# A fused top-k attention and two-MoE kernel: w_k loaded into w_v's later buffers, first loads on two queues, stand-in values from ScalarE

## The chip, the core and the metric

The kernel runs on one core of a Trainium2 chip. A core has five engines that work side by side: PE (TensorE, matrix products; PEld is its weight load), DVE (VectorE), ACT (ScalarE), POOL (GpSimd) and SP (SyncE, which here only issues DMAs). Each engine runs its own instructions strictly in order and waits on semaphores for the others. The metric is the device time in microseconds, the median of several runs.

## What is computed

```python
# 1. attention with top-k 32:  q, k, v are (4, 8, 576, 64)
scores = scale * q @ k.T                      # 576 scores a row
kth    = the 32nd largest of each row
attn   = softmax(where(scores >= kth, scores, -1e9)) @ v
# 2. x = attn as (4, 576, 512); each token is mixed with the one before it (mu_k, mu_r)
r, kk = sigmoid(xr @ w_r), relu(xk @ w_k) ** 2        # w_k 512x1024, w_v 1024x512, w_r 512x512
x = r * (kk @ w_v)
# 3. a routed MoE: each token goes to one of 8 experts (w1[e] 512x1024, w2[e] 1024x512)
out[b, s] = p[e] * (relu(x[b, s] @ w1[e]) @ w2[e])
```

w_k, w_v and w_r come as 64-bit floats; the kernel turns them into two 32-bit parts itself.

## The kernel before

The 2,304 tokens are 18 tiles of 128. A tile has 8 heads, worked off as 4 pairs of heads, so there are 72 **pairs** (`pair`, from L480). One pair with its two heads a = 0, 1 goes: PE scores (L511 or L516), ACT copies them out of PSUM (L498), DVE finds the eight largest of each of 8 blocks of 72 (L534) and three rounds of candidates (L544, L547); that gives an approximate threshold. Then the exact one is settled. DVE counts the scores below it into `sm` and writes the 0/1 mask `mk` (`cn`, L566). POOL does two things (`rp`): L570 writes eight **stand-in values** behind the mask (2^24 where a fixed number in `pick` exceeds the count, else 0), and L571 multiplies scores and mask. DVE takes the eight largest of these 584 numbers (`rx`, L575), and the eighth is the threshold whatever the count was. The stand-ins thus fill up the places that the count left open. ACT makes the final mask (L581), POOL subtracts it (L585), ACT takes exp (L589), PE transposes (L612), ACT copies (L615), PE multiplies with v (L625).

Between the pairs stand the first MoE (`mix`, `moe`; L823 to L947, in groups of two tiles) and, at the beginning, the conversion of the weights (`narrow`, from L684): 20 pieces of 128x512 64-bit numbers, 512 KB each, 8 of w_k, 4 of w_r, 8 of w_v. One piece is a DMA on SP's queue (L735) into a buffer `rw`, of which there are two, which it shares with other work; two ACT operations on it (L696, L711), four of DVE (L699 to L708), one or two of POOL, three PE products and two ACT copies into the final `wk` or `wv` buffer. There are eight `wk` and eight `wv` buffers.

After the pairs comes the second MoE (`slots`, up to L1826): a routing on DVE, PE and POOL (L1359), gathers of token rows by POOL (L1720), transposes (L1734), ACT and DVE splits into `xk` (L1737, L1740), expert products (L1758 or L1768, then L1808), with expert weights split into two parts by ACT, DVE and POOL (L1699, L1697, L1702), and scatters of the results (L1819).

What sets the order: every operation is handed to a planner (`Sched`, L35 to L143) with an estimated duration, a priority and the buffers it needs. It plays the program through with these estimates and emits each engine's instructions in the order in which they would start. The tables SHIFT, SLOPE and SCALE (L240 to L317) change priorities and durations by kind of operation; a kind is named by engine and function (`"ACT pair.ex"`). On the chip an engine keeps the emitted order, so an operation that is late holds up all behind it. While PE has nothing to do in the first 150 planned microseconds the planner puts in small products of no use (L1856), which keep PE running.

Of the kernel before, what the change touches and what calls it, by code (L numbers as in the profile page):

```python
# [146 lines left out]
def kernel(  # L147
# [92 lines left out]
    SHIFT = {"ACT Routing.own.<lambda>": 1600.4, "ACT keys.hi": -8273.1, "ACT mix.o1": -201.7, "ACT mix.o3": -55.0,  # L240
             "ACT moe.ev": -9550.0, "ACT moe.hi": -95.1, "ACT moe.rc": 2604.1, "ACT moe.rl": -1080.6,
             "ACT moe.sig": 9217.2, "ACT moe.sq": -2233.7, "ACT narrow.hi_": -6878.4, "ACT narrow.lo_": -3354.4,
             "ACT narrow.o1": -12605.5, "ACT narrow.o4b": 7243.4, "ACT narrow.o8": 82.5, "ACT pair.<lambda>": -3944.7,
             "ACT pair.cnt": 213.0, "ACT pair.cp": 153.5, "ACT pair.ev": -1356.5, "ACT pair.ex": 943.6,
             "ACT pair.ex2": 235.0, "ACT pair.nm": 645.5, "ACT pair.rl": -2339.7, "ACT queries.hi": -1850.3,
             "ACT slots.fin": -1800.3, "ACT slots.rl": 1990.9, "ACT slots.thi": -2317.5, "ACT slots.xhi": -8276.7,
             "ACT split.hi": 4421.4, "ACT x0_t.cs": -8538.1, "ACT x0_t.ev": -41.7,
             "DVE Routing.__init__.<lambda>": -8985.9, "DVE Routing.own.<lambda>": -2828.9,
             "DVE Routing.place.<lambda>": 1634.7, "DVE Routing.place.counts": -7047.9,
             "DVE Routing.place.order": 5600.6, "DVE Routing.place.rows": 2003.5, "DVE keys.lo": -172.9,  # L250
             "DVE mix.o1": 544.4, "DVE mix.o2": -1964.2, "DVE moe.lc": -7257.5, "DVE moe.lo": 12.5,
             "DVE moe.xs": 162.4, "DVE narrow.o1b": -1351.0, "DVE narrow.o2": 483.8, "DVE narrow.o3": 375.2,
             "DVE narrow.o4": -257.8, "DVE narrow.o9": 203.0, "DVE pair.cands": 3976.7, "DVE pair.ch": -3687.6,
             "DVE pair.cn": -78.5, "DVE pair.nm": -41.5, "DVE pair.r1": -646.5, "DVE pair.rx": -109.0,
# [1673 lines left out]
```

## Time and profile before

| | |
|---|---|
| median of 3 runs | 1061.44 us (1056.66 to 1063.55) |
| profiled execution | 1057.62 us, its span 1055.8 us |
| busy in the span | PE 988.2, DVE 880.2, ACT 778.6, POOL 754.4 us |
| pairs | from about 22 us (first L534) to about 700 us |
| routing of the second MoE | about 722 to 800 us |

The span runs from the first to the last instruction; 1.8 us lie around it. "Busy" is the time in which an engine had at least one instruction running. Idle time of an engine matters only where that engine, or one that waits for it, sets the end.

### The profile page before, as it was taken

Reading aid. Unit: us, or ns where it says so; the run is one execution under the profiler, and the core shown is the slowest. Engines: PE = TensorE matmul, PEld = TensorE weight load, DVE = VectorE, ACT = ScalarE, POOL = GpSimd, SP = SyncE. Lnnn points to the kernel's source line nnn. Section 1 sums busy time; section 2 is a strip of 40 time slices with the busy share of each in tenths; the row PEclk is TensorE's granted clock in tenths of the full one; section 3 lists DMA queues with packets and bytes.
Section 4 is the critical chain, followed back from the end, with each engine's and each line's share of the span. In section 5 each row is a group of like instructions: output and inputs, shape, how many; then the busy total and the mean of one; then the engine's idle time right before and its main releaser. Section 6 shows DMA issues by size and latency. Waiting matters only on the chain.

```text
span 1055.8 us, 24502 instructions
## 1 busy us (share of the span) xinstructions
PE 988.2 (94%) x7790; PEld 827.2 (78%) x7790; DVE 880.2 (83%) x3589; ACT 778.6 (74%) x1763; POOL 754.4 (71%) x858
## 2 busy tenths in 40 slices
PE   7898998899999999999999999999859999999896
PEld 6687884678787788888888788877759889888784
DVE  4998997858999999999989999958695669777672
ACT  4776786976999989989989799885335566566452
POOL 2686986666898989989978899873356757566552
PEclk9999999999999999999999999999789999999898
DMA  7421123234212353221342211003813646666650
GB/s 182 123 56 54 54 62 96 62 82 104 61 44 70 93 132 81 49 66 37 91 103 70 66 42 41 22 1 112 287 51 116 226 150 230 217 206 202 207 182 19
DMA packets 100974, 109.49 MB, mean 104 GB/s; under 512 B 49374, under 2 KB 67806, under 8 KB 100832
## 3 DMA queue, kind: packets, MB, share of 16 engines
q1 hardware_dynamic: 97312, 97.32, 32.4%
q0 software_dynamic: 3520, 10.49, 2.9%
q8 instruction: 64, 1.05, 0.4%
q14 instruction: 78, 0.64, 0.2%
HBM read 76.57 MB, written 10.49 MB: 82 GB/s over the span
## 4 chain that ended last, share of the span: by engine, by line
PE 58%; DVE 21%; ACT 8%; DMA 6%; issue 4%; SPq 0%; POOL 0%; POOLq 0%; DVEq 0%; ACTq 0%
PE pv L1808 9%; PE pb L1758 9%; PE xa L625 6%; PE pv L916 5%; PE pb L888 5%; PE pb L612 5%; DVE c L534 4%; PE pb L516 4%; PE pb L823 3%; DVE c L575 2%; PE pb L1768 2%; DVE mk L566 2%; PE pb L511 2%; PE pv L1856 2%; DMA rw<-in_moe_w_k_dram 2%
## 5 line engine op out<-in xcount | busy, mean ns | idle before, releaser
L585 POOL TENSOR_TENSOR at<-s,at 128x576 f32<-128x576 f32 x144 | 205.0, 1435 | 31.0 <-ACT at L581 30.4
L571 POOL TENSOR_TENSOR mk<-s,mk 128x576 f32<-128x576 f32 x144 | 205.6, 1428 | 0.0
L534 DVE MAX8 c<-s 128x8 f32<-128x72 f32 x1152 | 166.5, 219 | 4.8 <-ACT s L498 4.8
L581 ACT ACTIVATE at<-s,TS 128x576 f32<-128x576 f32 x144 | 112.1, 783 | 16.2 <-DVE TS L578 15.8
L1758 PE MATMUL pb<-xk,wk 128*128 128x256 f32 x864 | 114.6, 289 | 7.2 <-DVE xk L1740 7.2
L1758 PEld LDWEIGHTS pb<-xk,wk 128*128 128x128 f32 x864 | 112.3, 196 | 10.7 <-DVE xk L1740 7.5
L575 DVE MAX8 c<-mk 128x8 f32<-128x584 f32 x144 | 108.4, 757 | 14.6 <-POOL mk L571 14.6
L589 ACT ACTIVATE at<-at,sm 128x576 f32<-128x576 f32 x144 | 113.0, 786 | 7.7 <-POOL at L585 7.3
L498 ACT ACTIVATE s<-pb 128x288 f32<-128x288 f32 (+1 forms) x320 | 110.1, 418 | 8.4 <-PE pb L516 4.5
L612 PE MATMUL pb<-ident,at 128*128 128x128 f32 x648 | 99.1, 281 | 17.0 <-ACT at L589 11.8
L566 DVE TENSOR_SCALAR_CACHE_REDUCE mk<-s,c 128x576 f32<-128x576 f32 x144 | 114.8, 801 | 0.0
L615 ACT ACTIVATE aT<-pb 128x384 f32<-128x384 f32 x216 | 98.5, 497 | 12.7 <-PE pb L612 12.1
L916 PE MATMUL pv<-wv,kk 128*128 128x512 f32 x384 | 106.5, 406 | 0.0
L888 PE MATMUL pb<-xk,wk 128*128 128x256 f32 x768 | 103.9, 286 | 0.0
L612 PEld LDWEIGHTS pb<-ident,at 128*128 128x128 f32 x648 | 74.0, 142 | 37.5 <-ACT at L589 17.7
L625 PE MATMUL xa<-aT,vb 128*64 128x128 f32 (+1 forms) x1600 | 98.6, 269 | 2.4 <-ACT aT L615 1.8
L888 PEld LDWEIGHTS pb<-xk,wk 128*128 128x128 f32 x768 | 95.2, 188 | 2.9 <-issue 1.4
L625 PEld LDWEIGHTS xa<-aT,vb 128*64 128x64 f32 x1600 | 80.8, 138 | 19.2 <-issue 11.1
L1808 PE MATMUL pv<-wv,vb 128*128 128x512 f32 x330 | 88.5, 402 | 0.9 <-ACT xT L1816 0.9
L516 PE MATMUL pb<-kT,qx 128*128 128x288 f32 x480 | 86.5, 314 | 1.4 <-DMA kT<-rw 0.8
L1702 DVE TENSOR_TENSOR wk<-s,wk 128x512 fp32r<-128x512 f32 x67 | 70.7, 1088 | 16.1 <-ACT wk L1699 8.9
L516 PEld LDWEIGHTS pb<-kT,qx 128*128 128x128 f32 x480 | 69.6, 188 | 13.3 <-issue 5.3
(258 smaller groups left out, 2232.1 us busy)
## 6 DMA issues: line engine op xcount, KB each, us to landing
s<-in_moe_w_dram SPq DMA_DIRECT2D x88, 256.0 KB, 4.1
kT<-in_moe_w_dram SPq DMA_DIRECT2D x44, 512.0 KB, 5.1
qx<-qh SPq DMA_DIRECT2D x112, 64.0 KB, 2.0
qx<-ql SPq DMA_DIRECT2D x112, 64.0 KB, 2.0
kT<-rw SPq DMA_DIRECT2D x48, 144.0 KB, 2.6
xd<-rr SPq DMA_DIRECT2D x18, 256.0 KB, 2.2
rw<-in_moe_w_k_dram SPq DMA_DIRECT2D x8, 512.0 KB, 4.8
qn<-in_q_dram SPq DMA_DIRECT2D x16, 256.0 KB, 3.1
```

The lines of the kernel that those rows point to most:

```text
L516: nc.tensor.matmul(dst(hf), qx.t[:, w, a, hp % 2, :], kt.t[:, a, c], start=(w == 0), stop=(w == 1))
L534: nc.vector.max(c8.t[:, a, c, :], s2.t[:, c * CH:(c + 1) * CH])
L566: nc.vector.tensor_scalar(mk.t[:, :S], s2.t, c8.t[:, a, NCH + 2, 7:8], 0.0, op0=OP.is_lt, op1=OP.add, accum_out=sm.t[:, 2 + a:3 + a])
L571: nc.gpsimd.tensor_tensor(mk.t[:, :S], s2.t, mk.t[:, :S], op=OP.mult)
L575: nc.vector.max(c8.t[:, a, 0, :], mk.t)
L585: nc.gpsimd.tensor_tensor(x, s2.t, x, op=OP.subtract)
L612: nc.tensor.transpose(pt.t[:, c * P:(c + 1) * P], at.t[:, (g * GB + c) * P:(g * GB + c + 1) * P], ident)
L625: nc.tensor.matmul(xa.t[a * D:(a + 1) * D, hp * P + p0:hp * P + p0 + n], vb[:, a, j, :], evs[c // GB][1].t[:, c % GB, p0:p0 + n], start=(j ...
L888: nc.tensor.matmul(pm.t[:, :N], WK[c][f // 4].t[:, x, f % 4 * P:(f % 4 + 1) * P], xk.t[:, y, c, :N], start=(m == 0), stop=(m == 3 * DC - 1))
L916: nc.tensor.matmul(pvs[ti].t, kk.t[:, x, ti * P:(ti + 1) * P], WV[f].t[:, y, :], start=(f == 0 and m == 0), stop=(f == FB - 1 and m == 2))
L1758: nc.tensor.matmul(ph.t[:, (f % 2) * N:(f % 2 + 1) * N], w[:, x], xt.t[:, y, c, :], start=(n == 0), stop=(n == 3 * DC - 1))
L1808: nc.tensor.matmul(py.t, hT.t[:, x, o_:o_ + P], w[0].t[:, y, :], start=(f == 0 and m == 0), stop=(f == FC - 1 and m == 2))
```

## The change

Four edits, one of them in the tables.

1. The 8 pieces of w_k no longer go through the two `rw` buffers. They are loaded into the eight `wv` buffers (`RAWK`), which get w_v's converted pieces later; each `wv` buffer is free for w_v when the conversion of its w_k piece has read it. The planner now takes 4.0 us (it was 2.3) for a `narrow` load to land.
2. Of the first loads, the first tile of q (L450) and the second head of the first two heads of k (L387, L388 for h = 1) are issued from ACT's queue; all others stay on SP's.
3. The stand-in values are no longer made by POOL but by ACT (`si`, L583): Relu(STAND - count * STAND / (pick - 0.5)), which is positive where the count is below `pick`, with STAND 2^40. The constants are made once by four small DVE instructions (L356 to L359). DVE's L588 (L575 before) now waits for both ACT's `si` and POOL's product.
4. SHIFT, SLOPE and SCALE have new numbers for nearly every kind of operation, so that the order of all engines is laid anew.

```diff
-    HUGE, STAND = 2.0 ** 100, 2.0 ** 24
+    HUGE, STAND = 2.0 ** 100, 2.0 ** 40
-    SHIFT = {"ACT Routing.own.<lambda>": 1600.4, "ACT keys.hi": -8273.1, "ACT mix.o1": -201.7, "ACT mix.o3": -55.0,
+    SHIFT = {"ACT Routing.own.<lambda>": 560.7, "ACT keys.hi": -7234.3, "ACT mix.o1": -201.7, "ACT mix.o3": -55.0,
...
     WK = [[new("wk", [P, 2, 512], F32R) for _ in range(2)] for _ in range(DC)]
+
+    RAWK = [new("wv", [P, 2, DM]) for _ in range(2 * DC)]
     WV = [new("wv", [P, 2, DM], F32R) for _ in range(FB)]
...
-    pick = wp.tile([P, 8], F32, name="pick")
-    nc.gpsimd.iota(pick, pattern=[[-1, 8]], base=S - TOPK + 8, channel_multiplier=0, allow_small_or_imprecise_dtypes=True)
+    pick = wp.tile([P, 9], F32, name="pick")
+    nc.gpsimd.iota(pick[:, :8], pattern=[[-1, 8]], base=S - TOPK + 8, channel_multiplier=0, allow_small_or_imprecise_dtypes=True)
+    nc.vector.tensor_scalar(pick[:, :8], pick[:, :8], -0.5, None, op0=OP.add)
+    nc.vector.reciprocal(pick[:, :8], pick[:, :8])
+    nc.vector.tensor_scalar(pick[:, :8], pick[:, :8], -STAND, None, op0=OP.mult)
+    nc.vector.memset(pick[:, 8:9], STAND)
...
+                e = nc.scalar if h and not (b or hp) else nc.sync
...
-                nc.sync.dma_start(qn.t[p0:p0 + n], q[b, :, s:s + n, :].rearrange("h p d -> p h d"))
+                (nc.sync if t else nc.scalar).dma_start(qn.t[p0:p0 + n], q[b, :, s:s + n, :].rearrange("h p d -> p h d"))
...
             def rp(a=a, s2=s2, mk=mk):
-                nc.gpsimd.tensor_scalar(mk.t[:, S:], pick, sm.t[:, 2 + a:3 + a], STAND, op0=OP.is_gt, op1=OP.mult)
                 nc.gpsimd.tensor_tensor(mk.t[:, :S], s2.t, mk.t[:, :S], op=OP.mult)
+
+            def si(a=a, mk=mk):
+                nc.scalar.activation(mk.t[:, S:], pick[:, :8], AF.Relu, bias=pick[:, 8:9], scale=sm.t[:, 2 + a:3 + a])
...
-            o = sc_.op("POOL", 1.5, rp, [o], T0 + 4.6 + d, [], [s2, mk, sm])
-            o = sc_.op("DVE", 0.68, rx, [o], T0 + 6.2 + d, [], [mk, c8])
+            o2 = sc_.op("ACT", 0.2, si, [o], T0 + 4.6 + d, [], [mk, sm])
+            o = sc_.op("POOL", 1.4, rp, [o], T0 + 4.6 + d, [], [s2, mk])
+            o = sc_.op("DVE", 0.68, rx, [o, o2], T0 + 6.2 + d, [], [mk, c8])
...
-        raw = new("rw", [P, 2, S])
+        far = src is w_k
+        raw = RAWK[2 * c + f0 // n] if far else new("rw", [P, 2, S])
...
+        ld.lat = 4.0
```

Lines of the changed kernel lie 10 to 15 further down (L534 is L544, L575 is L588, L735 is L749, L1740 is L1755).

What the new order does at three places. First, SP's queue at the start of the program (`rw` and `wv` are the load buffers of the conversion, qn, kn, vb those of q, k and v). Before:

```order
1 L735 DMA rw<-in_moe_w_k_dram 128x1024 x2
2 L440 DMA qn<-in_q_dram 128x8x64
3 L1270 DMA wg_sb<-in_moe_w_gate_dram 128x4x8
4 L1271 DMA wg_sb<-in_moe_w_local_dram 128x4x1
5 L1272 DMA mu_sb<-in_moe_mu_k_dram 128x4x1
6 L1273 DMA mu_sb<-in_moe_mu_r_dram 128x4x1
7 L440 DMA qn<-in_q_dram 128x8x64
8 L735 DMA rw<-in_moe_w_k_dram 128x1024
9 L377 DMA kn<-in_k_dram 64x5x64
10 L378 DMA kn<-in_k_dram 64x4x64
```

Now:

```order
1 L749 DMA rw<-in_moe_w_r_dram 128x1024 x2
2 L749 DMA wv<-in_moe_w_k_dram 128x1024 x6
3 L1285 DMA wg_sb<-in_moe_w_gate_dram 128x4x8
4 L1286 DMA wg_sb<-in_moe_w_local_dram 128x4x1
5 L1287 DMA mu_sb<-in_moe_mu_k_dram 128x4x1
6 L1288 DMA mu_sb<-in_moe_mu_r_dram 128x4x1
7 L450 DMA qn<-in_q_dram 128x8x64
8 L749 DMA wv<-in_moe_w_k_dram 128x1024 x2
9 L387 DMA kn<-in_k_dram 64x5x64
10 L388 DMA kn<-in_k_dram 64x4x64
```

Three loads of 512 KB stood ahead of the first keys; now ten do, two of w_r first.

Second, POOL where the first token rows of the second MoE are gathered (`rr` is the gathered tile, wk and wv the expert weights' low parts). Before:

```order
683 L1702 TENSOR_TENSOR wk<-s_12179,wk 128x512
684 L1702 TENSOR_TENSOR wk<-s_12180,wk 128x512
685 L1702 TENSOR_TENSOR wk<-s_12181,wk 128x512
686 L1720 DMA rr<-xd,gi 128x512
687 L1702 TENSOR_TENSOR wk<-s_12185,wk 128x512
688 L1702 TENSOR_TENSOR wk<-s_12186,wk 128x512
689 L1720 DMA rr<-xd,gi 128x512
```

Now:

```order
542 L1717 TENSOR_TENSOR wk<-s_12133,wk 128x512
543 L1717 TENSOR_TENSOR wk<-s_12134,wk 128x512
544 L1735 DMA rr<-xd,gi 128x512 x2
545 L1717 TENSOR_TENSOR wk<-s_12135,wk 128x512
546 L1735 DMA rr<-xd,gi 128x512 x2
```

The first gather has two weight instructions ahead of it in place of three, and the second follows it directly. The second reuses the first one's buffer in both kernels, so it waits for the first tile's transposes on PE.

Third, DVE in the second placement of the routing, where the next block's `xk` is due (at, qx, rw, mk are the routing's work tiles). Before:

```order
1350 L1359 TENSOR_TENSOR at<-at,qx 128x576
1351 L1359 TENSOR_SCALAR rw<-mk,qx 128x128 x2
1352 L1359 TENSOR_TENSOR at<-at,rw 128x18x32
1353 L1359 TENSOR_SCALAR rw<-mk,qx 128x128 x12
1354 L1740 TENSOR_TENSOR xk<-pb,xk 128x4x128
1355 L1359 TENSOR_SCALAR rw<-mk,qx 128x128 x2
1356 L1740 TENSOR_TENSOR xk<-pb,xk 128x4x128
```

Now:

```order
1359 L1374 TENSOR_TENSOR at<-at,qx 128x576
1360 L1374 TENSOR_SCALAR rw<-mk,qx 128x128 x2
1361 L1374 TENSOR_TENSOR at<-at,rw 128x18x32
1362 L1755 TENSOR_TENSOR xk<-pb,xk 128x4x128 x2
1363 L1374 TENSOR_SCALAR rw<-mk,qx 128x128 x12
```

Both `xk` now stand ahead of the twelve `rw` instructions and not behind them.

## Rows read from the trace of the kernel before

**Rows 1.** Page, busy times, and the chain that ended last by engine.

```profile
PE 988.2 (94%) x7790; PEld 827.2 (78%) x7790; DVE 880.2 (83%) x3589; ACT 778.6 (74%) x1763; POOL 754.4 (71%) x858
...
PE 58%; DVE 21%; ACT 8%; DMA 6%; issue 4%; SPq 0%; POOL 0%; POOLq 0%; DVEq 0%; ACTq 0%
```

**Rows 2.** Stages: start:end, length, busy us of each engine, PE clock, DMA.

```profile
0.00:25.00 25.00, 19.33 (x208) 15.89 (x209) 10.79 (x41) 11.82 (x22) 5.66 (x18) 1.00 0.71 181
25.00:150.00 125.00, 116.42 (x1322) 97.69 (x1320) 117.61 (x520) 90.39 (x200) 95.83 (x99) 0.96 0.26 72
150.00:250.00 100.00, 91.46 (x683) 68.49 (x681) 75.88 (x344) 77.90 (x180) 62.33 (x72) 0.97 0.34 83
250.00:700.00 450.00, 436.12 (x3617) 363.65 (x3617) 431.56 (x2221) 409.05 (x987) 401.88 (x476) 1.00 0.26 66
...
784.00:800.00 16.00, 8.99 (x66) 8.90 (x67) 11.84 (x29) 1.28 (x4) 6.85 (x6) 0.68 0.34 108
```

**Rows 3.** Waits, whole span: who waited for whom; us, times, longest.

```profile
ACT xT L696 <- DMA rw<-in_moe_w_k_dram: 16.0, 8, 4.2
DVE c L575 <- POOL mk L571: 14.6, 9, 2.7
POOL mk L570 <- DVE mk L566: 13.4, 18, 1.9
```

**Rows 4.** Timeline, first 25 us: start, length, engine, instruction, [idle before].

```profile
0.75 0.89 SPq L735 DMA_DIRECT2D rw<-in_moe_w_k_dram  x2
4.66 0.67 ACT L696 ACTIVATE xT<-rw 128x512 f32<-128x512 f32 x1 [2.63 <-DMA rw<-in_moe_w_k_dram]
6.00 0.66 ACT L696 ACTIVATE xT<-rw 128x512 f32<-128x512 f32 x1 [0.67 <-DMA rw<-in_moe_w_k_dram]
16.27 0.63 PE L391 MATMUL pb<-ident,kn 128*128 128x128 f32 x4 [2.39 <-DMA kn<-in_k_dram]
20.35 0.67 ACT L696 ACTIVATE xT<-rw 128x512 f32<-128x512 f32 x1 [2.70 <-DMA rw<-in_moe_w_k_dram]
22.35 2.25 DVE L534 MAX8 c<-s 128x8 f32<-128x72 f32 x16 [0.21 <-ACT s L498]
```

**Rows 5.** Groups by line and shape, whole span: busy, mean ns, idle before.

```profile
L570 POOL TENSOR_SCALAR mk<-pick,sm 128x8 f32<-128x8 f32 x144 | 50.6, 351 | 19.8 <-DVE mk L566 13.4 <-DVE TS L578 5.8
L396 ACT ACTIVATE rw<-pb 128x64 fp32r<-128x64 f32 x12 | 2.7, 225 | 0.2
```

**Rows 6.** Groups, 250 to 700 us, ACT: the final mask.

```profile
L581 ACT ACTIVATE at<-s,TS 128x576 f32<-128x576 f32 x108 | 84.6, 786 | 8.7 <-DVE TS L578 8.2
```

**Rows 7.** Timeline, routing: POOL's gathers and the smallest ACT instruction.

```profile
741.49 1.21 POOL L1720 DMA_INDIRECT rr<-xd,gi  x1 [4.10 <-PE pv L875]
748.26 0.98 POOL L1720 DMA_INDIRECT rr<-xd,gi  x1 [2.49 <-PE pb L1734]
...
758.01 0.23 ACT L1359 ACTIVATE mk<-mk 128x32 f32<-128x32 f32 x1 [0.33 <-DVE mk L1359]
```

**Rows 8.** Timeline, routing: PE.

```profile
747.37 0.60 PE L1734 MATMUL pb<-ident,rr 128*128 128x128 f32 x4
747.73 2.31 PE L875 MATMUL pv<-wv,kk 128*128 128x512 f32 x9
752.32 0.84 PE L937 MATMUL pb<-ident,rr 128*128 128x128 f32 x4 [2.28 <-DVE rr L929]
754.66 1.08 PE L1734 MATMUL pb<-ident,rr 128*128 128x128 f32 x4 [1.50 <-DMA rr<-xd,gi]
757.10 5.47 PE L1758 MATMUL pb<-xk,wk 128*128 128x256 f32 x24
...
791.01 2.72 PE L1758 MATMUL pb<-xk,wk 128*128 128x256 f32 x11 [7.17 <-DVE xk L1740]
```

**Rows 9.** Timeline, second placement: DVE.

```profile
782.36 7.07 DVE L1359 TENSOR_SCALAR rw<-mk,qx 128x128 bf16<-128x128 bf16 x12
789.35 0.68 DVE L1740 TENSOR_TENSOR xk<-pb,xk 128x512 fp32r<-128x512 f32 x1
```

More of the change, by code (lines that the diff above doesn't have):

```diff
@@ L239 @@
              "rr": 3, "xT": 2, "sm": 13, "rw": 2, "wk": 8, "wv": 8}
-    SHIFT = {"ACT Routing.own.<lambda>": 1600.4, "ACT keys.hi": -8273.1, "ACT mix.o1": -201.7, "ACT mix.o3": -55.0,
[L241 to L254, printed above, removed]
-             "DVE pair.th": -290.3, "DVE queries.lo": 1224.6, "DVE slots.tlo": 1053.5, "DVE slots.xlo": -1378.6,
-             "DVE split.hi": 5962.0, "DVE split.lo": -1691.1, "DVE kernel.nmu": -4805.2,
-             "DVE kernel.ok_in": 1377.0,
-             "DVE kernel.ok_out": -2597.9, "DVE x0_t.nrm": -3136.3,
[6 rows of a table removed]
-             "POOL Routing.place.<lambda>": 5051.1, "POOL Routing.pool.consts_": -4153.1, "POOL mix.o1": 921.0,
-             "POOL mix.o4": 110.0, "POOL moe.lo": 4123.7, "POOL moe.sq": -133.5, "POOL narrow.o5": 8398.3,
-             "POOL narrow.o5r": -256.8, "POOL narrow.o6": -5082.6, "POOL narrow.o9": -14.0, "POOL pair.nbias": 3171.8,
-             "POOL pair.rp": 446.6, "POOL pair.sp": -4172.9, "POOL slots.gx": 794.9, "POOL slots.sca": 6498.8,
-             "POOL slots.tlo": -5777.7, "POOL split.lo": -834.2, "POOL x0_t.edge": 1874.6, "SP dma.go": 763.5,
-             "SP dma.keys": 1140.5, "SP dma.kspread": 10261.3, "SP dma.qspread": -8740.8, "SP dma.queries": 686.5,
-             "SP dma.raw": -11550.7, "SP dma.small": 912.7, "SP dma.vals": 3870.3, "SP load.go": -7105.4,
-             "SP moe.<lambda>": -2208.6}
@@ new lines @@
+    SCALE = {"ACT mix.o1": 1.25, "ACT moe.rc": 1.027, "ACT moe.rl": 1.036, "ACT narrow.o1": 1.094,
+             "ACT narrow.o4b": 1.179, "ACT pair.ex": 1.121, "ACT pair.si": 1.1, "ACT queries.hi": 1.177,
+             "ACT slots.fin": 1.026, "ACT slots.rl": 1.244, "ACT slots.thi": 1.141, "ACT x0_t.cs": 1.029,
+             "DVE mix.o2": 1.026, "DVE moe.lc": 0.925, "DVE moe.lo": 0.976, "DVE narrow.o2": 1.666,
+             "DVE narrow.o3": 1.242, "DVE pair.cands": 1.148, "DVE pair.ch": 0.931,
+             "DVE kernel.ok_in": 2.57,
@@ L734, in hl @@
             return [dst.t[:, k, :] if own else dst[:, k, c, f0:f0 + n] for k in range(2)]
-        ld = dma([lambda: nc.sync.dma_start(raw.t.rearrange("p a s -> p (a s)")[:, :2 * n].bitcast(I32), src[c * P:(c + 1) * P, 2 * f0:2 * (f0 + n)])], 1.5, prio - PAR['ra'], [raw], kind="raw")
+        ld = dma([lambda: nc.sync.dma_start(raw.t.rearrange("p a s -> p (a s)")[:, :2 * n].bitcast(I32), src[c * P:(c + 1) * P, 2 * f0:2 * (f0 + n)])], 1.5, prio - PAR['ra'], [raw], kind="rawk" if far else "raw")
+        ld.lat = 4.0
         o = sc_.op("ACT", 0.52, o1, [ld], prio, [nq], [raw])
```

86 lines of the change are left out of this document (54 added, 32 removed), and 24 rows, old and new, of tables (SHIFT, SLOPE).

## The prediction

> **What bounds the kernel now.** I read the page's busy times and its chain of waits first, then the table by stages, then who waits for whom, and last the timelines of the two places where the table shows holes. PE is busy 94% of the span and makes 58% of the chain that ended last; DVE makes 21%, ACT 8%, DMA 6%, POOL nothing [rows 1]. The stages say more [rows 2]. From 250 to 700 us, in the pairs with the first MoE between them, PE is busy 436.1 of 450 us, DVE 431.6, ACT 409.1, POOL 401.9: four engines nearly full, none with over 11% to give. The reader is to see that there is no large gain in this stage, whatever is taken off one engine: DVE idles 18.4 us there, and its work stays as it is. Before that the holes are larger: DVE idles 14.2 us in the first 25, 7.4 from there to 150, and 24.1 from 150 to 250. The other holes lie in the routing of the second MoE, where PE waits for single instructions [rows 8].
>
> **The change, part by part.** The sum is made against the profiled execution (1057.62 us). It stands 3.8 below the median of the runs shown (1061.44), and inside their spread.
>
> *w_k in the `wv` buffers.* ACT waited 16.0 us for w_k's loads, in eight waits [rows 3], because a piece could be loaded only when one of two buffers was free. With eight buffers all eight are under way from the start. ACT loses those waits, but the work of the pairs is paced by DVE, and DVE idles only 7.4 us from 25 to 150 us. So the bounds are 0 and -7.4; I take -4, about the middle, since half of those holes need not come from loads.
>
> *First loads.* Ten loads of 512 KB now stand ahead of the first keys on SP, three before. The first two pieces arrived 1.34 us apart (ACT started on them at 4.66 and 6.00) [rows 4], so the tenth is there at 4.66 + 9 x 1.34 = 16.7 us, and with two q tiles of half that size (0.67 each) and the keys themselves the first keys are there at about 18.6, an estimate from these rows; before they were there at 16.27. Having the second head's keys on ACT's queue doesn't help, as the scores need the whole `kT`, and the first head's are on SP. From keys to the first L534 it took 6.1 us, of which ACT stood 2.70 waiting for a piece of w_k [rows 4]. That wait is gone: the first L534 comes between 18.6 + 3.4 = 22.0 and 18.6 + 6.1 = 24.7, against 22.35. I take +1.5 (bounds -0.4 and +2.4), nearer the late end, because ACT has conversions in front of the scores. The four DVE instructions on the constants stand where DVE idles: 0.
>
> *150 to 250 us.* Here w_v and w_r still go through the two `rw` buffers, but w_k no longer does, and the planner places their first use 1.7 us later. Of DVE's 24.1 us idle I take -3. A new order can also open a hole: bounds -10 and +5.
>
> *Stand-ins off POOL.* 144 x 0.351 = 50.6 us leave POOL [rows 5]. POOL has no share in the chain, so most of it is worth nothing; what counts is that DVE stood nine times, 14.6 us, waiting for POOL's product [rows 3], and the product now starts 0.35 us earlier: 9 x 0.35 = 3.2. I take -2 (bounds 0 and -14.6, if POOL's whole backlog goes).
>
> *Stand-ins on ACT.* The trace has no 128x8 ACT instruction. The nearest rows are 0.23 us for 128x32 [rows 7] and 0.225 for 128x64 [rows 5]. I take 0.22: 144 x 0.22 = 32 us, of which the pair stage gets 108 [rows 6], 24 us. ACT idles 41 there, so 17 are left: it fits. What it costs is that ACT, which also empties PSUM, gets as full as DVE (433 of 450). I take +2; the bounds are 0 and the rival below. `si` also waits for DVE's count; queued behind it on ACT are score copies (L498) and masks, for which DVE and POOL wait.
>
> The Trainium skill speaks against this edit ("ScalarE: Activation LUTs", section Rules for kernel authors): relu belongs on VectorE, and an ACTIVATE is to be budgeted at about 0.3 us plus 0.83 ns per element. By that it would be 144 x 0.307 = 44 us, 33 of them in the pair stage, an estimate from that page, and the cost term would be some 2 us more; the trace's 0.23 us for a wider instruction is under it.
>
> *Routing, first gathers.* The second tile's gather started at 748.26 after a wait for the first tile's transposes at 747.37, its own transposes ran at 754.66 after waiting, and the expert products began at 757.10 [rows 7, 8]. The new order takes two weight instructions from between the gathers, and DVE writes the row indices ahead of the weighting factors. The second gather still needs the first's buffer, so the chain of two gathers stays; only its start moves. I take -3 (bounds +1 and -6).
>
> *Routing, second placement.* PE stood 7.17 us for `xk` [rows 8], which stood behind twelve instructions of 7.07 us on DVE [rows 9]. Now `xk` is ahead of them. What is late next: the placement's 18 products on PE need those twelve. DVE is through with them at about 782.4 + 1.3 + 7.1 = 790.8; PE has 24 expert products and 3 others to do first, about 5.5 us at the pace of row 757.10, less at full clock, so it waits 1.5 to 3.5 us there. Gain 3.6 to 5.6; I take -4 (bounds 0 and -7.2). PE's granted clock was 0.68 from 784 to 800 [rows 2], behind that wait; I count nothing for it.
>
> The rest of the second MoE is laid anew too, but PE is full in nearly all of it, and its work is the same: 0, give or take 4.
>
> Sum: -4 + 1.5 - 3 - 2 + 2 - 3 - 4 = -12.5, so 1045.1 for an execution like the profiled one. The median shown lies 3.8 above that one; I add half of it, 1.9: **1047**, with 1038 to 1056 as this case's own range.
>
> **The rivals.**
> *DVE covers everything.* The pairs are paced by a DVE that is 94 to 96% full, so freed ACT waits and POOL time vanish, and only the routing gains, part of it given back at the 18 products: -4, so 1055.5. For it: the 94% from 25 to 150 us. Against it: the 24 us idle after 150.
> *More of everything.* The hole from 150 to 250 closes by 10, DVE's waits for POOL go by 7, and the clock in the routing stays up: -24, 1035.5. For it: these holes are there in the table. Against it: something else fills up, as a rule.
> *ACT becomes the bound.* `si` stands in order behind DVE's count. POOL's instruction waited for that count 18 times, 0.74 us each [rows 3]. The 17 us that ACT has left are used up by 23 such waits, one in five of the 108. If one in four waits, ACT is occupied 409 + 24 + 20 = 453 us in this stage, and if no engine can be filled above DVE's 431.6 / 450 = 95.9%, the stage takes 472, +22. With the start (+1.5) and the routing (-7) that is +16.5: 1076. Against it: the planner knows of the wait and places `si` behind the count.
> *The loads stay in the way.* Ten loads at once bring the keys later than 20 us, and the waits for w_k turn into waits for keys and v: +4.5 at the start and the -4 lost, 1055.5 again.
>
> **How the numbers follow.** Within 1%, about what a measurement here can tell from no change, is 1050.8 to 1072.1. Chances: the forecast 0.42, DVE covers it 0.27, more of everything 0.14, ACT the bound 0.11, loads in the way 0.06. Faster by over 1%: four fifths of the first, the third and a little of the second, 0.51. Slower by over 1%: the ACT case, 0.11. The rest, 0.38. The range 1031 to 1064 leaves out the ACT case and the far end of the third.
>
> **What would show it.** In the changed profile: no wait of ACT for w_k's loads worth naming; the first L544 between 22 and 25 us; DVE idle from 25 to 250 near 24 us, 31.5 before; L583 at about 0.22 us each and ACT near 433 of the 450 us of the pair stage; POOL about 39 us emptier there; PE waiting under 4 us at the second placement. The forecast is wrong if the pairs end no earlier than 695 us while ACT's idle time before `si` is over 20 us, or if a new wait of PE in the routing takes the place of the one removed.

## The result, and the profile after

The changed kernel takes **1071.4 us** (median; 1069.1 to 1073.7) against 1060.8 for the kernel before (four runs, 1056.7 to 1063.6): a ratio of 1.0103, 95% interval 1.0062 to 1.0144. It is about 1% slower; the forecast was 1047, the range 1031 to 1064. The profiled execution took 1070.4 us with a span of 1068.5, 12.7 longer than before. The last pair's L587 (the section on the change calls this line L588) starts at 708.82 us, L575 at 697.72 before, so 11.1 of the 12.7 are lost by the end of the pairs and 1.6 behind them. Before, then now:

```profile
697.72 0.77 DVE L575 MAX8 c<-mk 128x8 f32<-128x584 f32 x1 [2.65 <-POOL mk L571]
```

```profile
708.82 0.77 DVE L587 MAX8 c<-mk 128x8 f32<-128x584 f32 x1 [0.89 <-POOL mk L580]
```

These are single executions. In six runs below that keep the pairs' order of before and take no measurably longer (x4_before_wk, x5_before_first_wk, d3_act_copy, z1_swap, z2_first_swap, f2_best) the last L575 starts at 700.6 to 707.8 us, so that this split is known to some 5 us only.

Page after, busy times and the chain that ended last, to be read beside [rows 1]:

```profile
PE 991.4 (93%) x7727; PEld 824.9 (77%) x7727; DVE 884.5 (83%) x3593; ACT 813.5 (76%) x1907; POOL 703.8 (66%) x714
...
PE 55%; DVE 18%; ACT 16%; issue 4%; DMA 3%; POOL 2%; SPq 0%; ACTq 0%; DVEq 0%; POOLq 0%
```

PE and DVE have nearly the same work as before, POOL has 50 us less, ACT 35 more, and ACT's share of the chain is 16% where it was 8%. The stages of the changed kernel, columns as in [rows 2]:

```profile
0.00:25.00 25.00, 14.69 (x169) 13.54 (x169) 6.04 (x18) 8.16 (x13) 4.12 (x15) 0.85 0.83 261
25.00:150.00 125.00, 118.01 (x1308) 97.49 (x1309) 121.87 (x561) 100.92 (x239) 89.65 (x80) 0.99 0.19 51
150.00:250.00 100.00, 87.93 (x642) 65.70 (x641) 74.54 (x331) 80.20 (x184) 57.96 (x58) 0.91 0.31 79
250.00:700.00 450.00, 433.97 (x3564) 360.35 (x3563) 419.73 (x2182) 423.76 (x1068) 355.83 (x358) 0.99 0.27 68
```

DVE's work done is the third busy figure. It is 4.8 us behind at 25 us, level at 150 (127.9 us done, 128.4 before), 1.8 behind at 250 and 13.7 behind at 700. So the start was late and was made up; in these two traces the loss within the pairs comes from 250 to 700 us, where DVE now idles 30.3 us, 18.4 before, and ACT is the fuller of the two. Who waits for whom from 150 to 710 us (us, times, longest), to be read beside [rows 3]: now, then before, then the group of the new instruction over the whole span:

```profile
POOL at L597 <- ACT at L593: 41.1, 38, 4.2
...
DVE c L544 <- ACT s L508: 10.8, 8, 3.5
DVE c L587 <- ACT mk L583: 9.9, 10, 2.9
...
DVE c L587 <- POOL mk L580: 3.0, 4, 0.9
```

```profile
POOL at L585 <- ACT at L581: 20.5, 22, 2.6
...
DVE c L534 <- ACT s L498: 4.6, 4, 2.4
```

```profile
L583 ACT ACTIVATE mk<-pick,sm 128x8 f32<-128x8 f32 x144 | 56.4, 404 | 7.8 <-DVE TS L590 4.0 <-DVE mk L576 3.4
```

DVE's wait for POOL's product (14.6 us before) has for the most part turned into a wait for ACT's stand-ins, and the two together are little shorter (12.9 us). What has grown is DVE's wait for ACT's score copies (10.8 us, 4.6 before) and POOL's for ACT's final masks (41.1 us, 20.5 before). Each stand-in lasts 404 ns where the forecast had 220, and ACT hardly stands idle ahead of it (7.8 us in all). The start, beside [rows 4]:

```profile
8.33 3.42 SPq L1287 DMA_DIRECT2D mu_sb<-in_moe_mu_k_dram  x1
...
12.42 3.24 SPq L450 DMA_DIRECT2D qn<-in_q_dram  x1
...
16.72 0.66 ACT L710 ACTIVATE xT<-wv 128x512 f32<-128x512 f32 x1 [4.62 <-DMA kn<-in_k_dram]
16.81 0.67 SPq L387 DMA_DIRECT2D kn<-in_k_dram  x1
...
23.61 1.09 PE L401 MATMUL pb<-ident,kn 128*128 128x128 f32 x4 [8.67 <-DMA vb<-in_v_dram]
30.32 2.29 DVE L544 MAX8 c<-s 128x8 f32<-128x72 f32 x16 [1.04 <-ACT s L508]
```

Two of SP's issues lasted 3.4 and 3.2 us, so that SP's first keys were only issued at 16.81 us, and ACT did no work for 4.62 us around its own two issues of keys, which lasted 0.62 and 0.56 us. The first L544 came at 30.32 us, 22.35 before. In the routing, beside [rows 8]:

```profile
768.46 1.76 PE L1773 MATMUL pb<-xk,wk 128*128 128x256 f32 x12
...
776.46 0.27 PE L1374 MATMUL pb<-ident,mk 128*18 128x128 f32 x1 [2.51 <-DVE mk L1374]
...
786.40 0.85 PE L1374 MATMUL pb<-ql,mk 128*128 128x144 f32 x2 [2.81 <-DVE ql L1374]
...
800.85 1.58 PE L1773 MATMUL pb<-xk,wk 128*128 128x256 f32 x12
802.27 0.32 PE L1374 MATMUL pb<-at,rw 128*128 128x64 bf16 x5
802.81 1.34 PE L1374 MATMUL pb<-at,rw 128*128 128x64 bf16 x8 [0.23 <-DVE rw L1374]
804.64 0.20 PE L1374 MATMUL pb<-at,rw 128*128 128x64 bf16 x1 [0.48 <-DVE rw L1374]
805.60 0.37 PE L1374 MATMUL pb<-at,rw 128*128 128x64 bf16 x2 [0.76 <-DVE rw L1374]
806.26 0.40 PE L1374 MATMUL pb<-at,rw 128*128 128x64 bf16 x2 [0.29 <-DVE rw L1374]
```

The wait of 7.17 us for `xk` is gone, and the 18 products wait 1.76 us for the `rw` in its place. Ahead of the placement PE now waits 2.51 us for `mk` and 2.81 us for `ql`; before, one wait of this kind was long:

```profile
770.20 1.30 PE L1359 MATMUL pb<-ql,mk 128*128 128x144 f32 x4 [3.30 <-DVE ql L1359]
```

### The profile page after: what moved, and what is told of

Its sections match the earlier page's. It is cut to its first block, busy times and chain, and to the rows that moved or that the text cites. A ratio compares the mean times of both kernels' runs of the same rounds, so it can differ in the third digit from the quotient of the medians.

```text
span 1068.5 us, 24522 instructions
## 1 busy us (share of the span) xinstructions
PE 991.4 (93%) x7727; PEld 824.9 (77%) x7727; DVE 884.5 (83%) x3593; ACT 813.5 (76%) x1907; POOL 703.8 (66%) x714
## 4 chain that ended last, share of the span: by engine, by line
PE 55%; DVE 18%; ACT 16%; issue 4%; DMA 3%; POOL 2%; SPq 0%; ACTq 0%; DVEq 0%; POOLq 0%
PE pb L1773 8%; PE pv L1823 7%; PE pv L931 6%; PE xa L638 5%; PE pb L903 5%; PE pb L838 5%; PE pb L625 4%; PE pb L526 4%; DVE c L544 3%; ACT at L601 2%; ACT s L508 2%; ACT at L593 2%; PE pb L1783 2%; PE pv L1871 2%; DVE c L587 2%
## 5 line engine op out<-in xcount | busy, mean ns | idle before, releaser
L580 POOL TENSOR_TENSOR mk<-s,mk 128x576 f32<-128x576 f32 x144 | 205.4, 1433 | 41.1 <-DVE TS L590 23.7
L544 DVE MAX8 c<-s 128x8 f32<-128x72 f32 x1152 | 165.8, 219 | 12.3 <-ACT s L508 11.8
L593 ACT ACTIVATE at<-s,TS 128x576 f32<-128x576 f32 x144 | 113.0, 785 | 13.4 <-DVE TS L590 12.9
L587 DVE MAX8 c<-mk 128x8 f32<-128x584 f32 x144 | 108.4, 757 | 13.4 <-ACT mk L583 9.9
L1717 DVE TENSOR_TENSOR wv<-kT,wv 128x512 fp32r<-128x512 f32 x86 | 68.7, 835 | 14.0 <-ACT wv L1714 11.9
```

Of the source, the lines that this page charges most:

```text
L544: nc.vector.max(c8.t[:, a, c, :], s2.t[:, c * CH:(c + 1) * CH])
L580: nc.gpsimd.tensor_tensor(mk.t[:, :S], s2.t, mk.t[:, :S], op=OP.mult)
L593: nc.scalar.activation(at.t[:, a * S:(a + 1) * S], s2.t, AF.Relu, bias=ts, scale=-HUGE)
```

## The experiments

Three theories stood against each other. **A**: the stand-ins on ACT cost, because ACT had less room than its idle time says. **B**: the new order costs, whoever writes the stand-ins. **C**: the late start is passed on to the end. An order that is laid out anew for each variant would differ in everything, so each variant below keeps the order of one of the two kernels on every engine and changes single instructions in it. Ratios are against the kernel before on the same chip, with 95% intervals; the changed kernel itself stands at 1.0103.

### In the changed kernel's own order

**e1_pool**: POOL writes the stand-ins again, ahead of its product.

```diff
-                nc.scalar.activation(mk.t[:, S:], pick[:, :8], AF.Relu, bias=pick[:, 8:9], scale=sm.t[:, 2 + a:3 + a])
+                nc.gpsimd.tensor_scalar(mk.t[:, S:], pick0, sm.t[:, 2 + a:3 + a], 2.0 ** 24, op0=OP.is_gt, op1=OP.mult)
```

> The changed kernel in its own order on every engine, but the stand-in values are written by POOL again, by the instruction of before, directly ahead of POOL's product. Theory A (the stand-ins filled ACT): ACT loses 56 us of busy time, 41 of them from 250 to 700 us, and DVE's waits of 9.9 us for L583 and 11.8 us for score copies (L508) fall to under 10 together. DVE idles 30 us in that stage now and 18 before, so the kernel gets 8 to 13 us faster: 1058 to 1063. Theory B (the order that the tables give is slower in the pairs, whoever writes the stand-ins): POOL's product is 0.35 us later 144 times, nothing is gained, 1069 to 1076. Theory C (only the late start costs): also no change, 1069 to 1073.

Measured: 1.0170 (1.0138 to 1.0201), 1076.4 us. Theory A missed here: ACT's busy time from 250 to 700 us fell to 402.2 us, less than the 409.1 of before, POOL's was 384.2 (401.9 before), and yet nothing was gained: the last L587 came at 714.8 us. From 150 to 710 us DVE now waits 21 times, 10.5 us, for POOL's product. That speaks for B, or for an order that is fitted to a product without the 0.35 us ahead of it; d4_pool_twice below shows how dear these are.

**e2_sp_queue** (all first loads issued by SP: `e = nc.sync`, twice) and **e3_keys_first** (first q tile and first keys issued ahead of all weight loads):

```diff
-        for o in order:
+        for o in sorted(order, key=lambda o: o.key not in (("SP dma.queries", 0), ("SP dma.keys", 0))):
```

> The changed kernel in its own order, but all first loads are issued by SP: the first tile of q and the second head of k at their planned places in SP's row. If the DMA issues on ACT delay the start (ACT stood from 12.1 to 16.7 us at them), ACT converts earlier, the keys come no later than now, and the first L544 comes at 28 us or earlier instead of 30.3. If the row of loads ahead on SP is the cause, SP has three more issues of 0.6 us, and the first L544 comes at 30 to 33 us, the time is 1070 to 1075.

> The changed kernel in its own order, but the first keys (both heads) and the first tile of q are issued ahead of all weight loads, on the same queues as in the change. Theory C (ten loads of 512 KB and their queue ahead of the keys make the start late, and this is passed on to the end): keys land before 6 us, the first L544 comes between 10 and 20 us instead of 30.3, and the time falls by at least the 8 us that the start lost, to 1063 or less. Theory A or B (the pairs are paced by full engines, the start is made up by the conversions anyway): the first L544 is early, but the conversions that stand between the pairs now hold the rest, and the time stays within 3 us of 1071.

Measured: 1.0128 (1.0095 to 1.0161) and 1.0114 (1.0077 to 1.0150). The second queue changes nothing to be measured (first L544 at 30.76 us without it). With the keys first, the first L544 came at 22.29 us, 8.0 earlier, and the time did not move: theory C falls. The first L544 came no earlier than that although the keys were issued at once: PE works through its row as it is laid, and the products of a conversion (L739 to L741) stand ahead of the keys' transposes, which ran at 17.56 us.

### In the order of the kernel before

**x3_before_act**: the same exchange the other way round, stand-ins on ACT and nothing else. **x4_before_wk**: only w_k in the `wv` buffers, the last five of its loads issued right behind the first keys. **x5_before_first_wk**: that, and first q tile and keys first. **x6_before_all**: w_k, second queue and stand-ins on ACT, without the new tables.

```diff
-                nc.gpsimd.tensor_scalar(mk.t[:, S:], pick, sm.t[:, 2 + a:3 + a], STAND, op0=OP.is_gt, op1=OP.mult)
+                nc.scalar.activation(mk.t[:, S:], pick[:, :8], AF.Relu, bias=pick[:, 8:9], scale=sm.t[:, 2 + a:3 + a])
...
-        raw = new("rw", [P, 2, S])
+        raw = new("rw", [P, 2, S]) if src is not w_k else sc_.buf("rw", lambda: sb.tile([P, 2, DM], F32, name="wv", tag="wv", bufs=8))
```

> The kernel before, in its own order on every engine, with the stand-in values written by ACT's Relu in place of POOL's instruction, at the place in ACT's row where POOL's product starts in the plan. The row of equal instructions on ACT gave 378 ns for this form, 288 ns of ACT's time each (13.8 us for 48): 41 us for all 144, 31 of them from 250 to 700 us, where ACT idled 41 us. Theory A (the edit itself is bad, by ACT's time and the waits behind DVE's count): 1065 to 1078. Theory B (the edit is worth little either way, the new order is what costs): 1054 to 1062.

> The kernel before, in its own order on PE, DVE, ACT and POOL, with the pieces of w_k in the eight wv buffers and the last five of their loads issued right behind the first keys. ACT's waits for w_k (16.0 us) go. By the prediction's step this is worth 4 us (0 to 7.4): 1050 to 1057 against 1057 for the kernel before. If the order of the other engines holds the conversions anyway, or the five loads are in the way of the first values (vb), there is no gain: 1056 to 1062.

> As the last, and the first tile of q and the first keys are issued ahead of all weight loads on SP's queue. If an early start is passed on to the end in this order, where the pairs stand nearer to the start, the first L534 comes before 18 us in place of 22.35 and the time is 1045 to 1053. If the conversions set the pace of the first 150 us, as keys loaded first left the changed kernel at the same time, it is within 3 us of the run with the w_k buffers alone.

> The kernel before, in its own order on the engines, with all three edits of the code and without the new tables: w_k in the wv buffers (five loads behind the first keys), the first tile of q and the second head of the first keys on ACT's queue, the stand-in values on ACT. Theory B (the new order is what costs): 1052 to 1062, well under the 1071 of the change. Theory A (the stand-ins on ACT cost): 1065 or more, near the change.

| | ratio | interval | last L575 |
|---|---|---|---|
| x3_before_act | 1.0161 | 1.0130 to 1.0192 | 715.3 us |
| x4_before_wk | 1.0024 | 0.9999 to 1.0048 | 702.5 |
| x5_before_first_wk | 1.0011 | 0.9989 to 1.0034 | 700.6 |
| x6_before_all | 1.0133 | 1.0102 to 1.0163 | 718.1 |

This settles it for the order of before: the stand-ins on ACT alone cost at least as much as the whole change, and w_k in the `wv` buffers gives nothing that can be measured, nor do keys that come first (in x5 the first L534 came at 20.2 us, where before 18 was expected). The second queue was tried by itself only in the changed order (e2_sp_queue). In x3_before_act DVE's work done is level with the kernel before at 150 us (128.4 us in both), 4.7 behind at 250 and 10.0 behind at 700: the delay grows all through the pairs, and the last L575 comes 17.6 us later. x4_before_wk did not take all of ACT's waits for w_k away (8.6 us of the 16.0 were left), and the start was 0.85 us earlier. x6 and the changed kernel (1.0133 and 1.0103, intervals overlap) can't be told apart, so no gain of the new tables shows.

### What the price on ACT is made of

**e7_probe**: rows of equal instructions.

> Leaves out the whole computation: it only runs rows of equal small instructions, none waiting for another engine, and writes zeros. ACT on 128x8: Copy; Copy with a scale per partition; Relu with a bias per partition; Relu with bias and scale per partition (the form of L583). If the duration of 404 ns belongs to the instruction's form, the last is near 400 ns and Copy near 0.2 us; if it is the neighbours in the kernel (a value that DVE has just written, a full engine), all four are near 0.2 us. DVE's and POOL's own form of the stand-in is there too: POOL near 351 ns, DVE under 0.2 us.

Groups of the row kernel (its own line numbers; busy us, mean ns of one; L25 is Copy, L27 Copy with a scale per partition, L31 Relu with bias and scale per partition, L39 DVE's form, L41 POOL's):

```profile
L31 ACT ACTIVATE t<-x,c 128x8 f32<-128x8 f32 x48 | 13.8, 378 | 0.0
...
L27 ACT ACTIVATE t<-x,c 128x8 f32<-128x8 f32 x48 | 9.4, 285 | 0.0
...
L41 POOL TENSOR_SCALAR t<-t,c 128x8 f32<-128x8 f32 x24 | 7.1, 325 | 5.0 <-DVEq L65 5.0
L25 ACT ACTIVATE t<-x 128x8 f32<-128x8 f32 x48 | 4.9, 193 | 0.0
...
L39 DVE TENSOR_SCALAR t<-x,c 128x8 f32<-128x8 f32 x24 | 3.3, 225 | 0.0
```

The 404 ns belong to the form: 193 ns, and 92 more for each of the two values per partition. The neighbours that the prediction used (128x64 and 128x32) were of other forms. Since neighbours in a row overlap, one costs 13.8 / 48 = 288 ns of ACT's time. (DVE's form took 225 ns, where under 200 was expected.)

**d1_act_free**, **d2_act_wait**, **d3_act_copy**: the complete kernel before, and beside POOL's stand-in one more instruction on ACT, whose result nobody reads: the Relu on constants, the Relu on the count, the bare Copy.

```diff
+                nc.scalar.activation(scr, pk[:, :8], AF.Relu, bias=pk[:, 8:9], scale=pk[:, 8:9])           # d1
+                nc.scalar.activation(scr, pk[:, :8], AF.Relu, bias=pk[:, 8:9], scale=sm.t[:, 2 + a:3 + a])  # d2
+                nc.scalar.activation(scr, pk[:, :8], AF.Copy)                                              # d3
```

> The kernel before, in its own order, complete as it is; in addition ACT runs, 144 times at the place where the stand-ins on ACT stood, a Relu of the same form that reads constants and writes a tile that nobody reads: it waits for nothing, and nobody waits for it. POOL still writes the stand-ins. If ACT's time is the price of the stand-ins on ACT (0.288 us each, 31 us of the 41 that ACT idled from 250 to 700 us), most of the 15 us comes with it: 1066 to 1076. If the waits are the price (ACT standing in order behind DVE's count, DVE behind ACT), ACT's idle time takes it: 1057 to 1062.

> As the last, but the added Relu reads the count that DVE has just written, as L583 does, so ACT waits for DVE's count; nobody waits for the Relu. If ACT's time is the price, the same as the last, within 3 us. If ACT's wait behind the count is the price, over 8 us more than the last. What is left between this one and the 1074.5 of the kernel before with the stand-ins on ACT is DVE's wait for ACT, less what POOL's relief gives.

> The kernel before, in its own order, complete as it is; the added instruction of ACT is now a Copy of 128x8 without a value per partition, 4.9 us for 48 in the row of equal instructions, 102 ns each, 15 us for 144, where the Relu with two such values had 288 ns and 41 us. If the price goes with ACT's time (12.4 us for 41 us, 0.3 us per us), it is 4.4 us: 1062. If it goes with the number of instructions (each breaks into ACT's row), it stays at 10 us or more: 1068 and up.

Measured: 1.0117 (1.0080 to 1.0155), 1.0129 (1.0087 to 1.0172) and 1.0005 (0.9979 to 1.0031). An instruction that waits for nothing and for which nobody waits costs three quarters of what the stand-ins on ACT cost in x3_before_act (12.4 of 17 us by the ratios; the intervals overlap); the wait behind DVE's count adds nothing that can be told apart. So in the order of before it is ACT's time. And 15 us of ACT's time cost nothing to be measured, where 41 us cost 12.4. By an even price the 15 would cost 4.5 us, and d3's interval (-2.2 to 3.3 us) leaves that out; with d1 at the lower end of its own interval (8.5 us) it would be 3.1. A price that starts only at some height is thus likely, but not shown. The stage from 250 to 700 us of d1_act_free, then of x3_before_act, then of d3_act_copy (columns as in [rows 2]; ACT's busy time is the fourth):

```profile
250.00:700.00 450.00, 432.92 (x3526) 359.58 (x3525) 423.81 (x2187) 421.72 (x1062) 389.32 (x463) 0.98 0.28 67
```

```profile
250.00:700.00 450.00, 432.81 (x3536) 359.44 (x3536) 426.22 (x2199) 420.17 (x1062) 356.35 (x358) 0.99 0.27 67
```

```profile
250.00:700.00 450.00, 436.19 (x3585) 364.66 (x3585) 431.28 (x2236) 410.20 (x1077) 395.73 (x471) 0.99 0.28 67
```

Over the whole stage ACT is equally full whenever it has the Relus: 423.8 us in the change, 418.9 to 424.2 in e2_sp_queue, e3_keys_first, x3_before_act, x6_before_all, d1_act_free and d2_act_wait, 94% at most, and the stage gets longer in place of ACT fuller. The size fits: 409 us of before [rows 2] and 108 x 0.288 = 31 are 440; at 424 per 450 us they need 467, 17 us more. In x3_before_act the pairs ended 17.6 us later than in the trace of before, in d1_act_free 16.5. This is no second proof, since the 424 are read from the same runs and the end of the pairs differs by up to 10 us between kernels that take the same time; the ratios above are the firmer measure. Nor are the 94% a limit of the engine. They are an average, and in a single stretch of the changed kernel ACT, the fourth figure, was busy 49.18 of 50 us:

```profile
350.00:400.00 50.00, 48.53 (x388) 40.01 (x388) 48.28 (x244) 49.18 (x130) 41.64 (x42) 1.00 0.43 103
```

With the bare Copy, 409 + 11 = 420 us of work are under those 424, and it cost nothing. (Its trace shows 410.2; it is that of its slowest execution, and 106 of the 108 Copies lie in the window.)

**h1_half**: the first head's stand-ins on ACT (`if a == 0`), the second's on POOL.

> The kernel before, in its own order, with the stand-ins of the first head of each pair on ACT and those of the second on POOL. If the price grows evenly, half of the 16 us of all of them: 1066. If POOL's relief counts first and ACT can take a part in its idle time, 1056 to 1062; this would be the version to look for.

Measured: 1.0046 (1.0021 to 1.0070), 1064.1 us: 4.9 us, less than half of x3's 17. But by the sum above it should have cost next to nothing (409 + 54 x 0.288 = 424.6), and by an even price (12.4 us for 41) 6.2, which its interval (2.2 to 7.4 us) holds. How the price grows between 15 and 41 us stays open. POOL's relief of 25 us, in any case, did not pay for it.

**f1_after_copy**: the changed kernel, with the stand-ins in a cheaper form of the same result.

```diff
-                nc.scalar.activation(mk.t[:, S:], pick[:, :8], AF.Relu, bias=pick[:, 8:9], scale=sm.t[:, 2 + a:3 + a])
+                nc.scalar.activation(mk.t[:, S:], pick[:, :8], AF.Copy, bias=STAND, scale=sm.t[:, 2 + a:3 + a])
```

> The changed kernel in its own order, with the stand-ins made by a Copy with a scale per partition and a constant added, in place of the Relu with scale and bias per partition. Where the Relu gave 0 it gives a large negative number, which is never among the eight largest; the result is the same. In the row of equal instructions this form took 285 ns against 378, and 196 ns of ACT's time against 288: 13 us less on ACT. By the prices so far (15 us of ACT's time: nothing; 41 us: 12.4) the 28 us that are left cost 6, so the changed kernel gets 5 to 7 us faster: a ratio of 1.003 to 1.006 in place of 1.010. If DVE's count and the order stand in the way and not ACT's time, it stays at 1.009 or more.

Measured: 1.0076 (1.0049 to 1.0102); L583 lasts 308 ns in place of 404, and the last L587 comes at 705.07 us in place of 708.82. The direction is the expected one, the size half of it, and the intervals overlap: in the changed kernel's own order ACT's time is a likely part of the cause, and by e1_pool not all of it.

### The same on the other engines

**d4_pool_twice**: the kernel before with POOL's stand-in twice. **d5_dve**: the kernel before with the stand-ins on DVE.

```diff
+                nc.gpsimd.tensor_scalar(scr, pick, sm.t[:, 2 + a:3 + a], STAND, op0=OP.is_gt, op1=OP.mult)            # d4
+                nc.vector.tensor_scalar(mk.t[:, S:], pick, sm.t[:, 2 + a:3 + a], STAND, op0=OP.is_gt, op1=OP.mult)    # d5, in rx
```

> The kernel before, in its own order, with POOL's stand-in instruction run twice, the second time into a tile that nobody reads, ahead of the product: POOL has 50.6 us more, and every product starts 0.35 us later. It is the mirror of what the change takes off POOL. The prediction took that at 2 us (0 to 14.6). If POOL has slack, 1058 to 1064; if POOL's 351 ns stand in the way of the pairs as much as ACT's, 1068 or more.

> The kernel before, in its own order, with the stand-ins written by DVE (compare and multiply, 128x8) directly ahead of its L575: 3.3 us for 24 in the row of equal instructions, 137 ns each, 20 us for all, 15 of them from 250 to 700 us, where DVE idled 18.4. If the fullest engine sets the pace and every instruction on it is paid in full: 20 us less what the earlier product gives (2 to 5), 1071 to 1078. If DVE's idle time of 14.6 us behind POOL's product takes a part, 1060 to 1068.

Measured: 1.0189 (1.0150 to 1.0228) and 1.0691 (1.0647 to 1.0735); the second is far outside of what was expected. The stage from 250 to 700 us of d4_pool_twice (POOL's busy time is the fifth), then DVE's and POOL's timeline in d5_dve:

```profile
250.00:700.00 450.00, 426.36 (x3473) 353.81 (x3472) 422.46 (x2160) 390.39 (x942) 411.46 (x558) 0.99 0.28 67
```

```profile
401.45 1.47 DVE L575 TENSOR_SCALAR mk<-pick,sm 128x8 f32<-128x8 f32 x1
401.47 1.42 POOL L571 TENSOR_TENSOR mk<-s,mk 128x576 f32<-128x576 f32 x1
402.84 1.42 POOL L905 TENSOR_TENSOR kk<-kr,kk 128x256 fp32r<-128x256 f32 x2
403.02 0.77 DVE L575 MAX8 c<-mk 128x8 f32<-128x584 f32 x1
...
406.93 0.18 DVE L575 TENSOR_SCALAR mk<-pick,sm 128x8 f32<-128x8 f32 x1
...
411.58 1.45 DVE L575 TENSOR_SCALAR mk<-pick,sm 128x8 f32<-128x8 f32 x1
411.60 1.40 POOL L585 TENSOR_TENSOR at<-s,at 128x576 f32<-128x576 f32 x1
```

POOL had 0% of the chain of before, and filling it costs no less than filling ACT: 402 + 108 x 0.32 = 437 us of work came out at 411.5 per 450 us, and the pairs ended 23.5 us later than in the trace of before. Two things are in this and were not told apart: POOL's time, and a product that starts 0.35 us later, for which DVE now waits 18.8 us in this stage (8.6 before). On DVE the instruction lasts 0.18 us when POOL is idle, and as long as POOL's product when that starts beside it; all 144 took 83.7 us, where 20 were expected.

### The routing step, and the best version

**z1_swap**: the kernel before, `xk` ahead of the twelve `rw` on DVE. **z2_first_swap**: that with x5_before_first_wk. **f2_best**: z1_swap with the first head's stand-ins on ACT in f1's form.

```diff
-        for o in order:
+        at = next((i for i, o in enumerate(order) if o.key == ('DVE slots.xlo', 3)), 0)
+        for o in sorted(order, key=lambda o: at + 0.5 if at and o.key[0] == 'DVE Routing.place.rows' and 8 <= o.key[1] <= 13 else order.index(o)):
```

> The kernel before with one thing of the new order: in the second placement of the routing DVE writes both xk ahead of the twelve rw instructions and not behind them. The prediction gave this 4 us (0 to 7.2): 1054 against 1058. PE's wait of 7.17 us ahead of the expert products goes; the placement's 18 products, which need the rw, wait in its place and start at 791.3 in place of 793.5 at best, so that 2 us may be all: 1056. If the clock of TensorE, 0.68 behind that wait, stays up, 2 us more.

> What the runs so far leave as the best version: the kernel before in its own order, stand-ins on POOL, w_k in the wv buffers, the first tile of q and the first keys issued first, and xk ahead of the twelve rw instructions. The early start alone gave nothing (a ratio of 1.0011), so by the pairs' pace only the routing counts: 1054 to 1057. If start and routing are both worth what the prediction gave them, 1048 to 1052.

> The kernel before with xk ahead of the twelve rw instructions (0.995 by itself), and the stand-ins of each pair's first head on ACT in the cheaper form: 14 us of ACT's time, as much as cost nothing. POOL loses 25 us. If POOL's relief is worth a part of what its doubling cost (20 us for 50), this is the fastest: 1045 to 1051. If it is worth nothing, as in the half with the Relu, 1055 to 1058, no better than the exchange on DVE alone.

Measured: **0.9951** (0.9926 to 0.9976), 0.9963 (0.9938 to 0.9988) and 0.9959 (0.9939 to 0.9978), medians 1055.5, 1054.3 and 1056.2 us. All three beat both kernels, by the same amount as far as can be told: in the order of before the exchange on DVE is worth some 5 us (2.5 to 7.8), the early start and POOL's relief (with 14 us more on ACT) nothing beside it. PE in z1_swap at that place, to be read beside the last row of [rows 8]:

```profile
790.92 1.56 PE L1758 MATMUL pb<-xk,wk 128*128 128x256 f32 x11 [0.56 <-DVE xk L1740]
792.33 0.54 PE L1359 MATMUL pb<-at,rw 128*128 128x64 bf16 x4
793.89 0.20 PE L1359 MATMUL pb<-at,rw 128*128 128x64 bf16 x1 [1.02 <-DVE rw L1359]
795.00 1.83 PE L1359 MATMUL pb<-at,rw 128*128 128x64 bf16 x13 [0.91 <-DVE rw L1359]
```

The 7.17 us are 0.56, and 1.93 are lost at the products, as the prediction's step had it (1.5 to 3.5).

## Why the prediction was wrong

The step that failed is the one on the **stand-ins on ACT**: "ACT idles 41 there, so 17 are left: it fits", counted at +2. In the order of before it cost 12.4 us by ACT's time alone (d1_act_free) and 17 with all that hangs on it (x3_before_act). Two things in it were wrong. The price of one was taken from rows of another form: 0.22 for 0.288 us of ACT's time. The larger one is the room: ACT's idle time was taken as free. Of the 41 us that it idled from 250 to 700 us, 11 more of work cost nothing (d3_act_copy, 15 in the whole span), 31 cost 12.4 us (d1_act_free, 41 in the whole span). The profile of before does not tell how much room there is. Its fullest stretch of 50 us has ACT at 47.38 us, 94.8%, which looks like a ceiling near the 424:

```profile
600.00:650.00 50.00, 48.36 (x404) 40.88 (x403) 49.00 (x265) 47.38 (x115) 47.28 (x55) 1.00 0.17 40
```

But the 49.18 us of the changed kernel, shown above, go over it, and h1_half cost 4.9 us with 424.6 us of work, which by this mark (426) would have fitted.

A second step failed behind the pairs. The prediction had -3 and -4 for the routing, and "its work is the same: 0, give or take 4" for the rest. From the start of the last L575 or L587 to the end of the span the changed kernel takes 359.7 us, and 359.0 to 363.2 in the five runs with its order, itself among them. The eleven with the order of before take 352.9 to 358.8 (355.8 in the mean; the trace of before itself 358.1), the three with the swap on DVE on top 349.2 to 354.6. So the new order takes some 5 us longer there although the swap is in it, where 7 less were forecast: about half of the 10.6 us that the change lost. The work is the same (from the first expert product on PE is busy 273.4 us, 272.8 before). The new order waits elsewhere, as for `mk` and `ql` above; that is a part of it, and where the rest goes was not followed up.

The rival "ACT becomes the bound" (1076, a chance of 0.11) was the nearest, and names the right place. Its number is in part luck: it had +22 in the pairs and -7 behind them, where the two traces show 11.1 and 1.6. Its mechanism, one wait in four behind DVE's count, was not it: ACT stood 7.8 us ahead of L583, and d2_act_wait adds nothing to be measured to d1_act_free.

Of the signs that the prediction named, four came near the forecast (no wait of ACT for w_k; POOL emptier by 46 us in the pair stage, 39 forecast; ACT at 424 there, 433 forecast; PE waiting 1.76 us at the second placement) and three did not (the first L544, L583's 404 ns, and DVE's idle time from 25 to 250 us, 28.6 where 24 were forecast). Of what was to show the forecast wrong, the pairs did end later than 695 us, but ACT's idle time ahead of L583 was 7.8 us and not over 20. The other steps, by their own numbers:

| step | forecast | the runs |
|---|---|---|
| w_k in the `wv` buffers | -4 (0 to -7.4) | ACT's waits for w_k gone, worth nothing: x4_before_wk 1.0024 |
| first loads | +1.5; first L544 at 22.0 to 24.7 | 30.32, out of the bounds; but the start decides nothing: e3_keys_first, x5_before_first_wk |
| 150 to 250 us | -3 | DVE did 1.3 us less there than before |
| stand-ins off POOL | -2 (0 to -14.6) | 0 for half of them, with 14 us more on ACT: f2_best beside z1_swap |
| first gathers | -3 (+1 to -6) | 0: 59.4 us from the last L575 to the first expert product before, 59.6 now |
| second placement | -4 (0 to -7.2) | -5 in the order of before: z1_swap 0.9951; no gain left in the new order |
| rest of the second MoE | 0, give or take 4 | with the two rows above +5, where -7 was forecast |

The first loads were mis-sized since the sum counted only how fast 512 KB land. What the rows of the start show is two long issues of SP's, and ACT without work around its own. That "the second head's keys on ACT's queue" do not help was right (e2_sp_queue). That the start is worth nothing was not foreseen by either sign: by 150 us DVE has done much the same work (125.8 to 128.4 us) whether its first maxima came at 22 us (e3_keys_first, before) or at 30 (the change).

What is not settled is the new order. Behind the pairs it loses more than the swap gives. In the pairs it stays as late with the stand-ins back on POOL (e1_pool, 1.017), although ACT and POOL are both emptier there than before, so that ACT's load is not all that holds it; the cheaper form on ACT gave 3 us (f1_after_copy). Whether the new order is worse in itself or only fitted to a POOL without stand-ins was not told apart. That the stand-ins on ACT cost 17 us is shown for the order of before; how much of the changed kernel's 1% is theirs is not.

## What to carry to other kernels

Where several in-order engines are 90% full side by side, none has the room that its idle time shows, and no single figure of the profile gave it here. Measure the price before moving work: add a dummy instruction of the same form, for which nobody waits, to the engine in its present order (d1_act_free, d3_act_copy), and price the instruction by a row of its own form. A share of 0% in the chain does not make an engine's time free (POOL: 50 us more, with its products later, cost 20), and taking 25 us off it paid nothing. A wait that is named, long and on the engine that ends last, as PE's 7.17 us for `xk`, was worth what the trace said in the order in which it was read; in an order laid out anew other waits took its place. So change the order of two instructions before moving work between engines.
